# Reordering the start of a fused retention and MLP kernel, and moving its crossbar transposes to another queue

## The chip, the cores and the metric

The kernel runs on one core of one Trainium2 chip. The metric is the device time of one execution in microseconds (us), given as the median of several executions of the same kernel. The profile is one execution, taken by the hardware profiler, and all times of day in it count from the start of its span. One thing is needed all through this study: the time of an execution is some 1.7 us more than its span. So spans are compared with spans here, and times with times.

## The reference

```python
def _attn_ref(q, k, v):                     # q, k, v: 8 batches x 8 heads x 576 x 64
    scores = scale * np.matmul(q, k.transpose(0, 1, 3, 2))
    gamma = 1.0 - 2.0 ** (-5.0 - np.arange(H, dtype=np.float32))
    Dmat = np.where(rel >= 0, gamma[:, None, None] ** rel[None, :, :], 0.0)
    return np.matmul(scores * Dmat[None, :, :, :], v)

def _moe_ref(x, w_in, w_out):               # 4608 x 512, 512 x 2048, 2048 x 512
    h = x @ w_in
    sp = np.where(h > 20.0, h, np.log1p(np.exp(np.minimum(h, 20.0))))
    g = h * np.tanh(sp)
    return (g @ w_out).astype(np.float32)
```

The output of the first function, with heads laid side by side, is the `x` of the second.

## The kernel before

Work comes in **chunks** of 128 tokens; two chunks are a **pair**, four are a **tile** of 512 tokens, and there are 36 chunks. The decay `gamma ** (i - j)` is split into a factor on q and one on v. For a chunk, VectorE scales q (step P), k is cast to bf16 (step C, GpSimd, first tile only), v is scaled (step V, GpSimd in the first tile, VectorE later), q and k are transposed (step T), TensorE makes the scores and VectorE multiplies them by the causal mask (step S), and TensorE multiplies them by v (step O). Then comes the MLP: `g1` multiplies a tile by one of 16 blocks of `w_in` into PSUM, ScalarE applies Mish, and `g2` multiplies by `w_out`.

The start, and the first tile's transposes:

```python
    def load_v(n, queue):
        (b, i0, _), = chunks[n]
        queue.dma_start(out=pairs[n // 2]["v"][:, n % 2], in_=v[b, :, ds(i0, P), :].rearrange("h p d -> p h d"))

    load_v(0, nc.scalar)
    load_v(1, nc.scalar)
    for n in range(NCH):
        load_first(n)              # q and k of chunks 0 to 3, on SyncE's queue
    ...
    keep_warm(13)                  # matmuls on zeros
    ...                            # constants, masks
    load_v(2, nc.gpsimd)
    load_v(3, nc.gpsimd)
    ...
    # step_v: GpSimd for the first tile
        (nc.gpsimd if early else nc.vector).tensor_tensor(r["vs"][:, u], r["v"][:, u], g, op=OP.mult)
    ...
    # step_t
        if n >= NPE:               # pairs 8 to 17: one crossbar transpose each
            nc.scalar.dma_start_transpose(out=r["qk"]..., in_=r["qks"]...)
            return
        if n < NCH:
            tp = ps_h.tile([P, 2, NP, P], BF16, name="hp")
            for i in range(2):     # q, then k
                lines = r["qks"][:, i, u].rearrange("p h d -> p (h d)")
                for t in range(4):
                    nc.tensor.transpose(tp[:, i, t, :], lines[:, ts(t, P)], ident)

                nc.scalar.copy(r["qk"][:, i, u]..., tp[:, i]...)
            return
    ...
    one(0, "PCVT")
    for n in range(NCH):
        last = n == NCH - 1
        keep_warm(4)
        if not last:
            one(n + 1, "P")
        one(n, "S")
        keep_warm(3)
        if not last:
            one(n + 1, "CV")
            if n < 2:
                load_w_in(2 * n, 2)
            one(n + 1, "T")
            one(n, "O")
    load_w_in(4, 4)                # the third piece: blocks 4 to 7 of w_in
    load_w_in(8, 4)
    ...
    for f in range(2):
        g1_some(0, f, NCH - 1)     # "the first projection": blocks 0 to 3, 128x384 matmuls
    one(3, "O")
    for f in range(2, 4):
        g1_some(0, f, NCH - 1)
    g1_chunk(3, 0)
    for i in range(4, nF):         # "block 4" and on: the first 128x512 matmuls
        ...
        g1(0, i)
```

The part near 126 us, in the third tile:

```python
    for i in range(nF):
        visit(6 + i // 8, i % 8)
        if i == 12:
            step_p(8)
            step_v(8)
        elif i == 14:
            cross(8)               # the first crossbar transpose
            load(11)
        g1(2, i)
        ...
```

## Time and profile before

| | before |
|---|---|
| time, median of 3 executions | 320.09 us (320.02 to 320.3) |
| span of the profiled execution | 320.1 us |
| TensorE busy | 306.9 us, 96% |
| first score matmuls | 9.02 us |
| first projection begins | 22.58 us |
| block 4 begins | 26.61 us |
| TensorE's longest wait after that | 2.19 us, at 127.96 |
| from the last matmul to the end | 3.32 us |

TensorE decides. It is nearly always busy once the first projection has begun, so what can be saved is the time before that, and single holes. The "block 4" row is the one to keep: everything before it is start, everything after it is an almost unbroken stream of matmuls, so what block 4 gains is what the start gains. Two more of the kernel before are used later: the stretch from 0 to 6 us (start and end, length, busy time of PE, PEld, DVE, ACT and POOL with counts, granted clock, share of transfer time, GB/s), and the durations in ns (shortest, median, longest) of the crossbar transposes on ScalarE's queue.

```profile
0.00:6.00 6.00, 4.45 (x13) 1.56 (x13) 3.09 (x27) 3.24 (x6) 3.92 (x16) 1.00 0.75 184
```

```profile
L268 ACTq DMA_TRANSPOSE qkT<-qks x10: 1332/1932/6815, 110.7 to 248.7; - x10
```

### The profile page before, as it was taken

The numbers are of one execution on the slowest core, as the hardware profiler recorded it, in microseconds if no ns is written. First come the engines' busy times: TensorE is split into PE (matmuls) and PEld (weight loads), VectorE is DVE, ScalarE is ACT, GpSimd is POOL, SyncE is SP. The second block draws the span as 40 slices with busy tenths as digits, with TensorE's granted clock in tenths as the row PEclk, the third lists the DMA queues.
The fourth block names the chain that finished last, engine by engine and source line by source line (L and its number), as shares of the span: only waits on it lengthen the run. The fifth ranks groups of instructions, "written<-read, shape, count | busy, mean of one in ns | idle before, by whom it ended". The sixth has DMA issues, their size and how long they took to land.

```text
span 320.1 us, 6094 instructions
## 1 busy us (share of the span) xinstructions
PE 306.9 (96%) x2649; PEld 160.1 (50%) x2649; DVE 131.9 (41%) x173; ACT 126.2 (39%) x208; POOL 82.1 (26%) x104
## 2 busy tenths in 40 slices
PE   6689999999999997999999999999999999999995
PEld 2345578745555553444545454445454544444444
DVE  4540555047647672353544444453535332001111
ACT  4347676412555541324434343434242422323200
POOL 6697573533440040404131312240000000000000
PEclk9999999999999999999999999999999999999999
DMA  8889999999997069597995959495040400000022
GB/s 205 213 126 226 200 202 218 203 217 236 223 245 114 16 148 156 124 181 134 211 174 123 168 127 186 112 174 125 33 100 33 100 33 35 33 34 35 33 77 87
DMA packets 73866, 43.38 MB, mean 136 GB/s; under 512 B 57712, under 2 KB 65136, under 8 KB 73840
## 3 DMA queue, kind: packets, MB, share of 16 engines
q0 software_dynamic: 43264, 25.69, 54.4%
q1 hardware_dynamic: 7552, 11.41, 11.5%
q10 hardware_dynamic: 23024, 5.90, 11.3%
q8 instruction: 20, 0.33, 0.4%
q14 instruction: 6, 0.05, 0.0%
HBM read 36.70 MB, written 9.44 MB: 144 GB/s over the span
## 4 chain that ended last, share of the span: by engine, by line
PE 90%; ACT 2%; DMA 2%; ACTq 2%; DVE 1%; SPq 1%; issue 0%; DVEq 0%
PE hp L370 33%; PE ops L408 31%; PE hp L408 6%; PE hp L393 4%; PE sc L306 3%; PE sc L355 3%; DMA qraw<-in_q_dram 2%; PE sc L348 2%; ACTq L268 2%; PE st L327 2%; PE ops L158 2%; PE sc L285 2%; PE hp L420 1%; SPq L138 1%; ACT qkT L286 1%; PE hp L381 1%
## 5 line engine op out<-in xcount | busy, mean ns | idle before, releaser
L370 PE MATMUL hp<-xT,w_in_t 128*128 128x512 bf16 x496 | 126.4, 380 | 2.2 <-ACT gT L372 2.2
L372 ACT ACTIVATE gT<-hp 128x512 bf16<-128x512 f32 x124 | 73.9, 598 | 131.7 <-PE hp L370 119.5
L408 PE MATMUL ops<-w_out_t,gT 128*128 128x512 bf16 x480 | 121.9, 379 | 0.0
L408 PEld LDWEIGHTS <-gT 128*128 128x128 bf16 x560 | 54.3, 98 | 64.6 <-issue 0.8
L428 DVE COPY res<-ops 128x512 f32<-128x512 f32 x30 | 20.8, 692 | 131.3 <-PE ops L408 131.3
L370 PEld LDWEIGHTS <-w_in_t 128*128 128x128 bf16 x496 | 46.0, 98 | 55.4 <-issue 3.0
L309 DVE TENSOR_TENSOR sm<-sc,mask 128x1024 bf16<-128x1024 f32 x36 | 42.7, 1218 | 20.5 <-PE sc L306 20.5
L535 POOL COPY seen<-qkT 1x1 bf16<-1x1 bf16 x10 | 1.8, 176 | 128.4 <-DMA qkT<-qks 128.4
L331 ACT ACTIVATE ssb<-st,diag 128x512 bf16<-128x512 f32 x32 | 20.2, 684 | 12.7 <-PE st L327 12.7
L359 DVE CAST xT<-sc 128x512 bf16<-128x512 f32 x32 | 20.8, 686 | 6.7 <-PE sc L355 5.9
L107 POOL DMA_DIRECT2D qraw<-in_q_dram x16 | 17.2, 1074 | 23.0 <-DVE qks L242 11.9
L259 DVE TENSOR_TENSOR vs<-vraw,gv 128x1024 bf16<-128x1024 f32 (+1 forms) x18 | 19.8, 1101 | 0.0
L242 DVE TENSOR_TENSOR qks<-qraw,gq 128x1024 bf16<-128x1024 f32 (+1 forms) x18 | 19.7, 1097 | 0.0
L408 PE MATMUL hp<-w_out_t,gT 128*128 128x512 bf16 x80 | 18.8, 380 | 0.0
L107 POOL DMA_DIRECT2D qks<-in_k_dram x16 | 17.3, 1083 | 5.2 <-DMA qraw<-in_q_dram 4.9
L107 POOL DMA_DIRECT2D vraw<-in_v_dram x16 | 17.4, 1090 | 3.7 <-DMA w_out_t<-in_moe_w_out_dram 1.6
L393 PE MATMUL hp<-xT,w_in_t 128*128 128x128 bf16 x272 | 16.7, 219 | 0.0
L286 ACT COPY qkT<-sc 128x1024 bf16<-128x1024 bf16 x12 | 12.1, 1014 | 11.7 <-PE sc L285 11.7
L393 PEld LDWEIGHTS <-w_in_t 128*128 128x128 bf16 x272 | 15.4, 98 | 0.7 <-issue 0.2
L355 PE MATMUL sc<-sm,vs 128*64 128x128 bf16 x288 | 13.8, 220 | 0.0
L158 PE MATMUL ops<-idle 128*128 128x512 bf16 x41 | 11.9, 424 | 1.3 <-DVE line L177 1.3
L306 PEld LDWEIGHTS <-qkT 64*128 64x128 bf16 x288 | 8.1, 94 | 9.6 <-issue 5.1
(68 smaller groups left out, 154.9 us busy)
## 6 DMA issues: line engine op xcount, KB each, us to landing
out_dram<-res SPq DMA_DIRECT2D x31, 256.0 KB, 3.3
qraw<-in_q_dram POOLq DMA_DIRECT2D x12, 512.0 KB, 6.6
vraw<-in_v_dram POOLq DMA_DIRECT2D x12, 512.0 KB, 9.7
qks<-in_k_dram POOLq DMA_DIRECT2D x12, 256.0 KB, 7.4
vraw<-in_v_dram POOLq DMA_DIRECT2D x10, 256.0 KB, 8.3
qraw<-in_q_dram POOLq DMA_DIRECT2D x8, 256.0 KB, 9.7
w_out_t<-in_moe_w_out_dram POOLq DMA_DIRECT2D x4, 512.0 KB, 11.9
qraw<-in_q_dram SPq DMA_DIRECT2D x8, 128.0 KB, 4.9
```

Source lines behind the costliest of these rows:

```text
L107: nc.gpsimd.dma_start(out=t[ds(off, ni)].rearrange("p u h d -> p (u h) d"), in_=src[ds(b, 2), :, ds(i0, ni), :].rearrange("b h p d -> p (b ...
L242: nc.vector.tensor_tensor(r["qks"][:, 0, u], r["q"][:, u], g, op=OP.mult)
L259: (nc.gpsimd if early else nc.vector).tensor_tensor(r["vs"][:, u], r["v"][:, u], g, op=OP.mult)
L309: nc.vector.tensor_tensor(sm.rearrange("p e n i -> p (e n) i"), sc.rearrange("p e n i -> p (e n) i"), (mask if len(chunks[n]) == 1 else ma ...
L331: nc.scalar.activation(ssb[:, :, :, e, :], st, AX.Copy, scale=diag[:, e:e + 1])
L355: nc.tensor.matmul(ot[ds(64 * e, 64), p, :], lhsT=vs[:, u, 2 * p + e, :], rhs=sm[:, e, p, :], start=(start and p == 0), stop=True, skip_gr ...
L359: (nc.scalar.copy if t == 0 else nc.vector.tensor_copy)(xts[t][:, :, ts(s, P)], ot)
L370: nc.tensor.matmul(hp, lhsT=w_in_t[:, c, ts(f, P)], rhs=xts[t][:, c, :], start=(c == 0), stop=(c == KC - 1))
L372: nc.scalar.activation(gts[t][:, f, :], hp, AX.Mish)
L393: nc.tensor.matmul(hp[:, j, :], lhsT=w_in_t[:, c, ts(4 * fb + j, P)], rhs=xts[t][:, c, ts(s, P)], start=(c == 0), stop=(c == KC - 1))
L408: nc.tensor.matmul(ops, lhsT=gts[t][:, f, ts(s, P)], rhs=w_out_t[:, f, :], start=(f == 0), stop=(f == nF - 1))
L428: copy(ot, ops)
```

## The change

Its intent is to shorten the start, by bringing q and k sooner and tightening the chain of each of the first chunks, and to free ScalarE's queue of crossbar transposes.

```diff
-    def load_v(n, queue):
+    def load_v(n):
...      # always nc.gpsimd now
-    load_v(0, nc.scalar)
-    load_v(1, nc.scalar)
...
-    keep_warm(13)
+    keep_warm(11)
...      # constants
+    load_v(0)
...      # masks
-    load_v(2, nc.gpsimd)
-    load_v(3, nc.gpsimd)
+    load_v(1)
...      # step_t
-            nc.scalar.dma_start_transpose(
+            nc.sync.dma_start_transpose(
...
                 for t in range(4):
                     nc.tensor.transpose(tp[:, i, t, :], lines[:, ts(t, P)], ident)
+            for i in range(2):
                 nc.scalar.copy(...)
...
-    one(0, "PCVT")
+    one(0, "PC")
+    load_v(2)
+    one(0, "VT")
     for n in range(NCH):
-        keep_warm(4)
+        keep_warm(3)
...
-        keep_warm(3)
+        keep_warm(2)
         if not last:
-            one(n + 1, "CV")
-            if n < 2:
-                load_w_in(2 * n, 2)
-            one(n + 1, "T")
+            one(n + 1, "C")
+            if n == 0:
+                load_v(3)
+            elif n == 1:
+                load_w_in(0, 2)
+            else:
+                load_w_in(2, 2)
+            one(n + 1, "VT")
             one(n, "O")
...      # third tile
-        if i == 12:
+        if i == 6:
             step_p(8)
             step_v(8)
-        elif i == 14:
+        elif i == 8:
             cross(8)
             load(11)
```

More of the change, by code (lines that the diff above doesn't have):

```diff
@@ L139, in load_first @@
                                   in_=heads[b, e, :, ds(i0, P), :].rearrange("p (g t) d -> g p (t d)", t=4))
-    def load_v(n, queue):
+    def load_v(n):
         (b, i0, _), = chunks[n]
-        queue.dma_start(out=pairs[n // 2]["v"][:, n % 2], in_=v[b, :, ds(i0, P), :].rearrange("h p d -> p h d"))
-    load_v(0, nc.scalar)
-    load_v(1, nc.scalar)
+        nc.gpsimd.dma_start(out=pairs[n // 2]["v"][:, n % 2], in_=v[b, :, ds(i0, P), :].rearrange("h p d -> p h d"))
     for n in range(NCH):
@@ L267, in step_t @@
         if n >= NPE:
-            nc.scalar.dma_start_transpose(out=r["qk"].rearrange("p i u n t -> p (i u n) t"),
+            nc.sync.dma_start_transpose(out=r["qk"].rearrange("p i u n t -> p (i u n) t"),
                                           in_=r["qks"].rearrange("p i u h d -> p (i u h d)"))
```

## The prediction

> **What bounds the kernel now.** I first read the page's busy shares and the row of slices: TensorE is busy 306.9 of 320.1 us, nine tenths or more in every 8 us slice but the first three (6, 6, 8 tenths) and the one from 120 us (7), at full granted clock. So only TensorE's idle time, and filler on it, can be gained. The view of waits for TensorE names that idle time:
>
> ```profile
> PE 306.9 (96%) x2649; PEld 160.1 (50%) x2649; DVE 131.9 (41%) x173; ACT 126.2 (39%) x208; POOL 82.1 (26%) x104
> ...
> PE hp L276 <- ACT qkT L278: 2.7, 4, 0.7
> PE hp L276 <- DVE qks L238: 2.4, 2, 1.4
> PE hp L370 <- ACT gT L372: 2.2, 1, 2.2
> PE ops L158 <- DVE line L177: 1.3, 1, 1.3
> ```
>
> The rest of that list is 1.3 us in pieces of at most 0.3. Behind the first two lines stand the first four chunks (up to 22.6 us, where the first projection starts); behind the third stands one event near 126 us. From 24.4 us on TensorE idles only 3.5 us until its last matmul at 316.8 us, 2.2 of them that event; then 3.3 us of final copy and store follow. The start is seen in the chain of waits of the first 24 us and TensorE's timeline there (start, duration, what):
>
> ```profile
> 4.12 6.57 DMA qraw<-in_q_dram
> ...
> 11.54 0.40 PE L276 MATMUL hp<-ident,qks 128*128 128x128 bf16 x4 [1.37 <-DVE qks L238]
> 12.61 0.38 PE L276 MATMUL hp<-ident,qks 128*128 128x128 bf16 x4 [0.67 <-ACT qkT L278]
> 12.92 0.41 PE L355 MATMUL sc<-sm,vs 128*64 128x128 bf16 x8
> 13.27 1.04 PE L158 MATMUL ops<-idle 128*128 128x512 bf16 x4
> 14.24 0.40 PE L306 MATMUL sc<-qkT 64*128 64x128 bf16 x8
> 14.57 0.82 PE L158 MATMUL ops<-idle 128*128 128x512 bf16 x3
> 15.23 0.39 PE L276 MATMUL hp<-ident,qks 128*128 128x128 bf16 x4
> ...
> 18.90 0.39 PE L276 MATMUL hp<-ident,qks 128*128 128x128 bf16 x4
> ...
> 22.58 1.46 PE L381 MATMUL hp<-xT,w_in_t 128*128 128x384 bf16 x8
> ```
>
> Chunk 1's q, issued at 4.12, lands only at 10.70: nothing but bytes ahead of it in the transfers. After that a chunk takes a fixed 3.68 us (15.23 to 18.90): eight transposes in two halves with a 0.67 us wait for the first copy, the output, seven idle matmuls, the scores. The event at 126 us is seen in ScalarE's timeline and TensorE's:
>
> ```profile
> 120.45 6.82 ACTq L268 DMA_TRANSPOSE qkT<-qks  x1
> 127.31 1.08 ACT L372 ACTIVATE gT<-hp 128x512 bf16<-128x512 f32 x2 [6.40 <-issue]
> 127.96 1.02 PE L370 MATMUL hp<-xT,w_in_t 128*128 128x512 bf16 x4 [2.19 <-ACT gT L372]
> ```
>
> ScalarE's queue sat 6.82 us on one crossbar transpose while a pair's loads ran; the activations behind it came late and TensorE ran out of PSUM. The other nine took 1.3 to 4.4 us and left no gap.
>
> **What the Trainium skill says.** *DMA: Bandwidth & Descriptors*, section "Issuing engines are not separate DMA queues": transfers from ScalarE, SyncE and GpSimd run on the same 16 engines and interleave. The trace agrees: v of chunks 0 and 1 (ScalarE's queue, landed 3.98 and 5.83) and v of 2 and 3 (GpSimd's, issued 3.08 and 4.12, landed 8.88 and 10.87) share the time with q and k from SyncE. So another queue makes no bandwidth; only the order counts. The same page, "Silent corruption: two transposing streams in flight at once", forbids mixing queues for transposes; all ten move together, so nothing is mixed (no run shows the corruption). *SBUF — State Buffer*, "Who interferes with whom": a VectorE tensor_tensor with both inputs in SBUF contends with GpSimd's reads. The trace shows q's scaling (128x512) at 0.69 us alone, 1.22 and 1.70 us beside GpSimd's v scaling. *TensorE: Matmul & The Clock Gate*, Part 1: the array starts at half clock until about 3.4 us of activity. The trace: idle matmuls 0.42 us apart from 1.26 to 4.23 us, about 0.22 after.
>
> **Part 1, loads of v.** By 10.7 us some 2 MB have been asked for ahead of or beside q of chunk 1: all four v (1 MB) and q, k of chunk 0 and q of 1 (0.75 MB), plus beginnings of k of 1. In the window 2.8 to 10.7 us that is about 260 GB/s. After: v0 first, v1 only after the masks (about 4 us), v2 and v3 after the casts of chunks 0 and 1. Ahead of q1 then stand q0, k0, v0, itself and a part of v1, about 1.15 MB: 4.4 us from 2.8, so about 7.2 us instead of 10.7. SyncE's issues of 0.65 us per half put q1's end of issue at 4.73, so it can't be much earlier. For chunk 0: q0 lands near 5, scaled at about 5.2 (VectorE's constants end at 5.26) against 6.02; k0 near 5.8 against 6.75. First scores at about 8.35 against 9.02. With the second half of chunk 1's transposes at 9.2 instead of 12.61, chunk 1's scores come at about 11.1 instead of 14.23.
>
> **Part 2, transposes ahead of copies, fewer idle matmuls.** New chunk, counted from its scores: scores 0.33, two idle 0.43, eight transposes 0.5, then output, which waits for the mask product: 0.44 + 1.22 + 0.05 = 1.7 after the scores began; output 0.34; three idle 0.65: 2.7. The other branch: transposes start at 0.76, end with latency at 1.4, both copies 2 x 0.59, release 0.17: 2.75. Both allow about 2.75 against 3.68. GpSimd's branch: cast 0.62, one DMA issue 0.9, v scaling 1.04 (1.49 when it meets VectorE): 2.6 to 3.0 a chunk, now nearly the same size. I take 2.75 to 3.0. Scores of chunk 3: 11.1 + 2 x 2.75..3.0 = 16.6 to 17.1 (21.59 before); first projection 0.87 later: 17.5 to 18.0 against 22.58, so 4.6 to 5.1 us earlier. The idle matmuls removed (10) are inside this sum, not beside it.
>
> **Part 3, can the weights keep up?** GpSimd's casts, scalings and issues end at about 5.8 + 4 x 0.62 + 4 x 1.04..1.25 + 4 x 0.9 = 16.0 to 16.9, where it issues the third w_in piece (18.38 before; it landed 5.4 us later, and was needed at 26.6). New landing 21.4 to 22.3; TensorE now wants it at 26.6 - 4.85 = 21.75. A stall of 0 to 0.5. Later loads come some 2 us earlier and TensorE 4.6 earlier, so each needs 2.6 us of slack: v of chunk 6 landed 40.04 for a scaling at 43.38 (3.3), v of 5 4.0, q of 5 and 6 5.4 and 4.6, the next pairs 9 us and more. So it holds, barely. **Start: 4.6 us gained.**
>
> **Part 4, crossbar transposes on SyncE's queue.** ScalarE is no longer blocked: the 2.19 us gap goes, also for a second reason: the first transpose and its load go from step 14 to step 8, so that load has landed before the second transpose. SyncE then sits on transposes, and stores behind it wait up to 7 us; a store comes every 6.9 us with three result buffers, so it costs nothing. The earlier scaling of pair 8 falls where VectorE idled 1.39 and 0.99 us between masks and copies; the copies come about 1 us later with 4.7 us until someone needs their buffers. **2.2 us gained.**
>
> Sum: 320.1 - 4.6 - 2.2 = **313.3 us**, 2.1% less.
>
> **Rivals.** (a) Transfers take over: w_in lands late. For it: transfers are busy eight or nine tenths from 0 to 96 us, and slack at the third piece is only 2.8 us plus what GpSimd gains. If GpSimd issues no earlier than before, the start gains only about 2.8: 315.1 us. Against it: GpSimd waited 5.0 us for k in the old start, which goes. (b) The pitch of a chunk becomes GpSimd's or VectorE's because the two collide on SBUF: 3.3 us instead of 2.8 costs 1 us: 314.3 us. (c) Transposes on SyncE block behind stores, arrive late, and the scores wait: up to 2 us at each of ten places. Against it: a transpose is issued ahead of its step's store and used some 9 us later, and took 4.3 us to land in most cases; unlikely. (d) The clock falls with fewer idle matmuls. Gaps of 1.37 us left no slow matmuls before (four transposes 0.40 us on both sides of it), and new gaps are shorter. (e) Better: casts begin sooner and the start gains 5.5: 312.4 us.
>
> **Range and chances.** The 2% line is 313.69 us, only 0.4 us above my number. Part 4 is nearly sure. The start carries the spread: plus 0.7, minus 2. I choose 313.3 with 312.2 to 315.2. Faster by over 2%: 0.55, because most of my cases (4.2 us or more at the start) fall on that side; within 2%: 0.44; slower: 0.01.
>
> **What the new profile would show.** q of chunk 1 scaled near 7.5 us, not 10.8; scores of chunks 1 to 3 at about 11.1, 13.9, 16.8; no wait of a transpose for a copy; the first projection near 17.7; GpSimd's third w_in issue near 16.5 and a wait of at most 0.5 us at the first 128x512 matmuls; no gap over 0.4 us after 24 us; ScalarE's 6.40 us hole gone; last matmul near 310. Wrong would be: TensorE waiting for w_in or for activations after it, transposes waiting for GpSimd's casts at every chunk, or gaps at scores of late pairs behind SyncE's queue.

## The result, and the profile after

The changed kernel took a median of **316.75 us** (316.62 to 316.85, 4 executions) against 320.05 (319.77 to 320.3) of the kernel before in the same rounds: ratio 0.9897, interval 0.988 to 0.9914. It is 1.0% faster, which at the 2% line counts as the same. A ratio here is the mean time of one kernel's fast runs over that of the other's of the same rounds, so it is not quite the ratio of the medians. Executions over 1.5% slower than the fastest of the same kernel are left out of the means.

| | before | after | predicted |
|---|---|---|---|
| span of the profiled execution, us | 320.1 | 315.1 | 313.3 |
| q of chunk 1 landed | 10.70 | 7.52 | 7.2 |
| k of chunk 0 landed | 6.75 | 6.81 | 5.8 |
| scores of chunks 0 to 3 | 9.02, 14.24, 17.92, 21.59 | 9.17, 12.30, 15.46, 18.32 | 8.35, 11.1, 13.9, 16.8 |
| first projection | 22.58 | 19.09 | 17.5 to 18.0 |
| third `w_in` piece issued, landed | 18.38, 23.80 | 18.27, 23.89 | 16.5, 21.4 to 22.3 |
| block 4 | 26.61 | 23.94 | 22.0 |

(The predicted 22.0 for block 4 is 26.61 less the 4.6 us.) TensorE's matmuls and their waits from 7 us on, after the change (start, duration, engine, line, what; in brackets the idle time before it and what ended it):

```profile
9.17 0.40 PE L305 MATMUL sc<-qkT 64*128 64x128 bf16 x8 [0.52 <-ACT qkT L277]
...
12.30 0.40 PE L305 MATMUL sc<-qkT 64*128 64x128 bf16 x8
...
13.23 0.87 PE L274 MATMUL hp<-ident,qks 128*128 128x128 bf16 x8
...
15.46 0.40 PE L305 MATMUL sc<-qkT 64*128 64x128 bf16 x8
...
19.09 1.46 PE L380 MATMUL hp<-xT,w_in_t 128*128 128x384 bf16 x8
...
23.94 1.90 PE L369 MATMUL hp<-xT,w_in_t 128*128 128x512 bf16 x8 [0.66 <-ACT gT L394]
```

The chunk's pitch fell to 3.13, 3.16 and 2.86 us, and from chunk 2 on the transposes run as eight in a row: no wait for the first copy is left between them. But the scores come 0.82 us late already at chunk 0, and the pitch is over the predicted 2.75 to 3.0 in two of three chunks. What sets it is seen on VectorE and GpSimd:

```profile
7.62 2.40 DVE L236 TENSOR_TENSOR qks<-qraw,gq 128x512 bf16<-128x512 f32 x1 [1.26 <-DMA qraw<-in_q_dram]
9.94 1.21 DVE L308 TENSOR_TENSOR sm<-sc,mask 128x1024 bf16<-128x1024 f32 x1
11.08 2.09 DVE L236 TENSOR_TENSOR qks<-qraw,gq 128x512 bf16<-128x512 f32 x1
13.09 1.21 DVE L308 TENSOR_TENSOR sm<-sc,mask 128x1024 bf16<-128x1024 f32 x1
14.23 1.80 DVE L236 TENSOR_TENSOR qks<-qraw,gq 128x512 bf16<-128x512 f32 x1
```

```profile
6.95 0.60 POOL L246 CAST qks<-kraw 128x512 bf16<-128x512 f32 x1 [1.48 <-DMA kraw<-in_k_dram]
7.50 0.89 POOL L143 DMA_DIRECT2D vraw<-in_v_dram  x1
8.41 1.05 POOL L257 TENSOR_TENSOR vs<-vraw,gv 128x512 bf16<-128x512 f32 x1
10.04 0.61 POOL L246 CAST qks<-kraw 128x512 bf16<-128x512 f32 x1 [0.58 <-DMA kraw<-in_k_dram]
...
15.40 1.09 POOL L246 CAST qks<-kraw 128x512 bf16<-128x512 f32 x1
...
18.27 1.54 POOL L123 DMA_DIRECT2D w_in_t<-in_moe_w_in_dram  x2
```

q's scaling, 0.69 us when alone, takes 1.80 to 2.40 us beside GpSimd's issue and scaling of v. From 7.62 us on, VectorE goes from scaling to mask to scaling without a pause, and the chain of waits of this execution runs over it from there to 17.2 us. GpSimd starts late: its first cast waits for k of chunk 0 until 6.95, where the prediction counted from 5.8, it waits 0.81 us more for k of chunks 1 and 2, and two casts take 0.80 and 1.09 us instead of 0.61. So the third `w_in` piece is issued no earlier than before, and lands 1.6 us or more after the predicted time. The 0.66 us in front of block 4 is put down to an activation in TensorE's row, but the weight load of the same matmul waited 0.83 us for `w_in`; the piece landed at 23.89, the matmul began at 23.94. Where nothing waits there, block 4 follows the first projection by 4.03 us (22.58 to 26.61 before); here it took 4.85.

The other half of the change did what was expected. ScalarE near the place of the old hole, the transposes on SyncE's queue, and TensorE's waits over the whole span (waiter and releaser: total us, times, longest):

```profile
119.38 0.60 ACT L371 ACTIVATE gT<-hp 128x512 bf16<-128x512 f32 x1 [1.13 <-PE hp L369]
122.29 0.60 ACT L371 ACTIVATE gT<-hp 128x512 bf16<-128x512 f32 x1 [2.31 <-PE hp L369]
```

```profile
L266 SPq DMA_TRANSPOSE qkT<-qks x10: 1317/1911/2003, 100.6 to 242.6; - x10
```

```profile
PE hp L274 <- POOL qks L246: 1.0, 2, 0.8
...
PE hp L369 <- ACT gT L394: 0.7, 1, 0.7
```

In this stretch every activation now waits for TensorE and not the reverse; no transpose holds a queue for more than 2.0 us; and the only 128x512 projection that waits is the one of the start.

From span to span the gain is 5.05 us where 6.8 was predicted. At block 4 it is 2.67 (26.61 to 23.94) instead of 4.6; after block 4 it is 2.53 instead of 2.2 (2.34 at the hole, 0.19 near 143 us); the end after the last matmul grew by 0.14 (3.32 to 3.46). But the medians differ by 3.3 us only. The profiled execution of the kernel before had a time of 321.84 us, 1.8 above that kernel's median, so its span of 320.1 is not the span of an execution of 320.09 us; that the two numbers look alike is chance. Of the eleven executions of that kernel which ran beside the first group of experiments, nine had spans of 317.5 to 318.6. The 5.05 us of the two profiles, less the 1.75 (321.84 less 320.09) by which the first of them was slow, are the 3.3 us of the medians.

### The profile page after: what moved, and what is told of

Same layout as the page of the kernel before. It is cut to its first block, busy times and chain, and to the rows that moved or that the text cites. A ratio compares the mean times of both kernels' runs of the same rounds, so it can differ in the third digit from the quotient of the medians.

```text
span 315.1 us, 6075 instructions
## 1 busy us (share of the span) xinstructions
PE 305.9 (97%) x2639; PEld 159.2 (51%) x2639; DVE 134.2 (43%) x173; ACT 126.3 (40%) x208; POOL 84.2 (27%) x106
## 4 chain that ended last, share of the span: by engine, by line
PE 91%; DVE 4%; ACT 1%; DMA 1%; SPq 1%; issue 1%; DVEq 0%
PE hp L369 34%; PE ops L407 32%; PE hp L407 6%; PE hp L392 4%; PE sc L305 3%; PE sc L354 3%; PE sc L347 2%; PE st L326 2%; DVE qks L236 2%; PE sc L284 2%; PE hp L419 1%; DVE sm L308 1%; DMA qraw<-in_q_dram 1%; SPq L138 1%; ACT qkT L285 1%; PE hp L380 1%
## 5 line engine op out<-in xcount | busy, mean ns | idle before, releaser
L107 POOL DMA_DIRECT2D qraw<-in_q_dram x16 | 17.2, 1076 | 15.2 <-DVE qks L240 7.1
L107 POOL DMA_DIRECT2D qks<-in_k_dram x16 | 17.2, 1079 | 8.3 <-DMA qraw<-in_q_dram 3.8
L354 PE MATMUL sc<-sm,vs 128*64 128x128 bf16 x288 | 13.9, 220 | 0.6 <-DVE sm L308 0.5
L305 PE MATMUL sc<-qkT 64*128 64x128 bf16 x288 | 11.9, 218 | 1.3 <-ACT qkT L285 0.8
```

What stands on the lines that cost most here:

```text
L107: nc.gpsimd.dma_start(out=t[ds(off, ni)].rearrange("p u h d -> p (u h) d"), in_=src[ds(b, 2), :, ds(i0, ni), :].rearrange("b h p d -> p (b ...
L305: nc.tensor.matmul(sc[:, e, p, :], lhsT=qk[r, 1, u, p, :], rhs=qk[r, 0, u, p, :], start=True, stop=True)
L354: nc.tensor.matmul(ot[ds(64 * e, 64), p, :], lhsT=vs[:, u, 2 * p + e, :], rhs=sm[:, e, p, :], start=(start and p == 0), stop=True, skip_gr ...
```

## The experiments

Each kernel was checked against the reference and timed beside the kernel before on the same chip. Where not said otherwise the result was correct. Before any of it ran, what each theory expects was written down. "Block 4" in the tables is when it began in the one profiled execution, and scatters by some tenths; the medians decide.

### Was the kernel before profiled in a usual execution, and what is each half worth?

Four kernels. In the texts, theory A is that the hole near 126 us is there in every execution, theory B that it was an accident of the profiled one. `again` is the kernel before, unchanged. `sp_only` and `early_only` are the kernel before with one half of the transposes' change each; `start_only` is the changed kernel with both halves taken back.

```diff
# sp_only, against before
-            nc.scalar.dma_start_transpose(
+            nc.sync.dma_start_transpose(
# early_only, against before
-        if i == 12:
+        if i == 6:
-        elif i == 14:
+        elif i == 8:
# start_only, against after: both of these undone
```

> The kernel before, unchanged. Its profiled execution took 321.84 us by the clock that times runs, against 320.05 in the median run, so its trace may hold something that most runs lack. Theory A (the 2.2 us hole near 126 us behind a crossbar transpose in ScalarE's queue comes in every run): span about 320.1 and the hole again. Theory B (the hole is an accident of the profiled execution): span 318.0 to 318.6, no gap of TensorE over 0.5 us near 126 us. Time in both 320.0, ratio 1.000.

> The kernel before with one word changed: the ten crossbar transposes from SyncE's queue instead of ScalarE's. Theory A: 2.2 us less, 317.8. Theory B: 0 to 0.7 us less, 319.4 to 320.0.

> The kernel before with pair 8 scaled and transposed at steps 6 and 8 instead of 12 and 14, transposes still from ScalarE. Theory A: the load of pair 11 lands before the second transpose, so the 2.2 us go here too, 317.8 to 318.5. Theory B: within 0.5 us of 320.0. If the early transpose meets the loads that still run near 100 us, a new hole instead: up to 322.

> The changed kernel with its start alone; transposes from ScalarE at the old steps. The traces of before and after put the start's gain at 2.66 us (24 us into the run). Expected by both theories 317.4, with 0.7 us (B) or 2.2 us and more (A) left to the changed kernel's 316.75 -- A can't hold if this gives 317.4 and the changed kernel 316.75.

| kernel | median us (range) | ratio to before, interval | block 4 | second transpose: start, us on the queue | hole behind it |
|---|---|---|---|---|---|
| again | 319.81 (319.48 to 320.05) | 0.9988, 0.9965 to 1.0012 | 25.28 | 119.12, 5.99 | 1.36 |
| sp_only | 318.36 (318.03 to 320.76) | 0.996, 0.9926 to 0.9995 | 25.66 | 118.61, 3.48 | none |
| early_only | 318.14 (318.08 to 318.47) | 0.9939, 0.9916 to 0.9962 | 25.79 | 119.62, 2.21 | none |
| start_only | 318.32 (317.61 to 319.19) | 0.9945, 0.9919 to 0.9971 | 24.47 | 118.30, 6.36 | 1.74 |

An execution of the kernel before can also start differently. In `again`, TensorE's wait at the hole, VectorE's scaling of q in chunk 1, and GpSimd's issue of the third `w_in` piece:

```profile
PE hp L370 <- ACT gT L372: 1.4, 1, 1.4
```

```profile
8.68 0.69 DVE L238 TENSOR_TENSOR qks<-qraw,gq 128x512 bf16<-128x512 f32 x1 [1.95 <-DMA qraw<-in_q_dram]
```

```profile
16.93 1.56 POOL L123 DMA_DIRECT2D w_in_t<-in_moe_w_in_dram  x2
```

q of chunk 1 is scaled at 8.68, not at 10.79 as in the execution that the prediction worked from, and block 4 starts 1.33 us earlier. That time scatters: with the same loads it was 9.38 in `sp_only`, 9.97 in `early_only` and 11.02 in `t_ahead` (below). So the prediction's late q is not a mark of that one execution, but it stands near the late end. The hole is no accident: it recurs in `again`, in `start_only` and in `t_ahead`, but as 1.36, 1.74 and 1.6 us, not 2.19. Either half of the transposes' change alone takes it away, so the two do the same work twice. The last two columns fit with that: at the early position the second transpose holds even ScalarE's queue for only 2.21 us; at the old position it holds SyncE's for 3.48 us, but there no activation stands behind it. By the medians a half is worth 1.5 to 1.8 us (319.9 to 318.36 and 318.14), the start is worth 1.6 (319.9 to 318.32), and the two add up to about the 3.3 us of the whole. Both theories had put `start_only` at 317.4; it missed that by 0.9 us, and three of its six executions have a mean clock of 0.993 to 0.995 (see rival (d) below).

### Theories of the late third piece and of the slow scalings

Four changes to the changed kernel. `w4_first` tests that GpSimd's late issue makes the piece late (theory G): it issues the third piece ahead of the last scaling of v. `v_dve` gives the first tile's v scaling to VectorE, so that only GpSimd's casts of k can still run beside q's scaling. `v_rows` loads v in rows of 1 KB (four times longer; the heads then come in a wrong order, relative error 0.57). Its output is wrong, which doesn't matter for the time. `idle_back` restores the number of idle matmuls.

```diff
# w4_first, against after
             else:
                 load_w_in(2, 2)
+                load_w_in(4, 4)
             one(n + 1, "VT")
...
-    load_w_in(4, 4)
# v_dve, against after
-        (nc.gpsimd if early else nc.vector).tensor_tensor(r["vs"][:, u], ...)
+        nc.vector.tensor_tensor(r["vs"][:, u], ...)
# v_rows, against after: load_v in two loads, as load_first does
+        for e in range(2):
+            nc.gpsimd.dma_start(out=...[:, n % 2, ds(4 * e, 4), :]..., in_=heads[b, e, :, ds(i0, P), :]...)
# idle_back, against after: keep_warm(11), (3), (2) back to 13, 4, 3
```

> The changed kernel with GpSimd issuing the third piece of w_in (the 1 MB one, needed by the fifth block of the first projection) right after the second, ahead of the last chunk's v scaling. Theory G (GpSimd's order sets when that piece lands, and it is what TensorE waits for at 23.9 us): the piece lands about 1 us earlier, TensorE's 0.66 us gap there goes, 316.1 us (ratio 0.9875). Theory P (the pace of the chunks alone sets the start): no change, 316.75 (0.9897), or the last chunk's output comes 0.8 us later and the time is 317.2.

> The changed kernel with the first four v scalings on VectorE instead of GpSimd. If it is the collision of GpSimd's v scaling with VectorE's q scaling on SBUF that stretches the latter from 0.69 to 1.8-2.4 us and so sets the 3.1 us pitch, q scalings fall to 0.7-1.3 us; GpSimd is free 1.05 us a chunk sooner, so the third piece of w_in is issued at 16 to 16.5 instead of 18.3 us. Theory G with collision: 315.0 to 315.5 us (ratio 0.985). Rival (transfers of k and v set the pace, k of chunk 3 lands at 14.7 whatever the engines do): start gains at most 0.7, 316.1.

> The changed kernel with v of the first four chunks loaded in 1 KB rows, as q and k are, instead of 256 B rows. The values then stand in the wrong places: a wrong result on purpose, the same bytes and the same work. In the trace a v of 256 KB holds up the stream 1.9 us against 0.7 for q or k. If rows and not bytes are the cost, k of chunk 0 lands at 5.7 instead of 6.8, k of chunk 3 at 11 to 12 instead of 14.7, GpSimd starts its chain 1.1 us earlier: third w_in piece at 17.1, 315.6 us (0.986). If only bytes count: no change. It issues eight loads from GpSimd instead of four, which costs up to 0.9 us a chunk of its time; that could eat the gain.

> The changed kernel with the idle matmuls of before (13, then 4 and 3 a chunk). If the removal gave time: 0.43 us a chunk on TensorE's own path, up to 1.7 us more, 318.4 (0.995). If TensorE waits for w_in at 23.9 us anyway, or the idle matmuls fill waits for VectorE: under 0.5 us, 316.8 to 317.2. If fewer idle matmuls let the clock fall in some executions (start_only's profile has a granted clock of 0.91 between 6 and 24 us), the spread shrinks and the clock is 1.000 in every run.

| kernel | median us (range) | ratio, interval | scalings of q, chunks 1 to 3 | third piece issued, landed | block 4 |
|---|---|---|---|---|---|
| after, first profile | 316.75 (316.62 to 316.85) | 0.9897, 0.988 to 0.9914 | 2.40, 2.09, 1.80 | 18.27, 23.89 | 23.94 |
| w4_first | 318.76 (317.39 to 320.81) | 0.9959, 0.9919 to 0.9999 | 2.17, 2.30, 2.23 | 17.67, 25.83 | 25.87 |
| v_dve | 316.82 (315.85 to 319.52) | 0.9896, 0.9853 to 0.994 | 0.69, 0.68, 1.10 | 16.02, 24.31 | 24.36 |
| v_rows | 316.9 (316.41 to 317.32) | 0.989, 0.9863 to 0.9918 | 0.69, 0.68, 2.44 | 17.82, 23.23 | 24.06 |
| idle_back | 317.7 (317.53 to 318.38) | 0.9919, 0.9892 to 0.9947 | 2.35, 2.43, 2.77 | 18.03, 23.86 | 24.70 |

`w4_first` missed: the piece was issued 0.6 us earlier and landed 1.9 us later, and TensorE waited 0.42 and then 1.68 us for `w_in`. So the time of issue does not decide by itself when the piece lands.

`v_dve` did what it should to the scalings, and nothing that shows to the time (its interval, 0.9853 to 0.994, would hide some tenths). Its scalings of q, then TensorE's first projection and block 4, and the transfer in the chain of waits over the first 25 us:

```profile
7.30 0.69 DVE L236 TENSOR_TENSOR qks<-qraw,gq 128x512 bf16<-128x512 f32 x1 [0.79 <-DMA qraw<-in_q_dram]
...
11.43 0.68 DVE L236 TENSOR_TENSOR qks<-qraw,gq 128x512 bf16<-128x512 f32 x1
```

```profile
18.99 1.46 PE L380 MATMUL hp<-xT,w_in_t 128*128 128x384 bf16 x8
...
24.36 1.90 PE L369 MATMUL hp<-xT,w_in_t 128*128 128x512 bf16 x8 [1.17 <-DMA w_in_t<-in_moe_w_in_dram]
```

```profile
16.02 8.29 DMA w_in_t<-in_moe_w_in_dram
```

The long scalings are gone, which shows that GpSimd's scaling of v made them long. Its issue of a load does not: in `v_rows` q of chunk 1 was scaled in 0.69 us from 7.59, beside an issue (7.38 to 8.46) and just ahead of the scaling of v (8.46), while in the changed kernel it began at 7.62, the scaling of v at 8.41, and it took 2.40. So about a tenth of a microsecond can decide whether the two meet. The pitch of chunks 2 and 3 became 2.82 us, as predicted. But that of chunk 1 was 3.71: there TensorE waited 1.00 us for the cast of k, which had landed at 10.23. The prediction worked out q of chunk 1, and not k. GpSimd issues the third piece at 16.02, even earlier than predicted, but the transfer then takes 8.29 us instead of the 5.62 of the changed kernel, and 1.17 us of waiting stands in front of block 4. By the trace's transfer records, 14 of the piece's 16 completions were in by 21.8 us and the last two came from 23.2 on; the trace does not name the transfer engines.

`v_rows` gives no sign that v's short rows are the cost: k of chunk 0 landed at 6.70, not at 5.7; its four additional issues could hide a small gain. `idle_back` is 0.8 to 0.9 us slower than `v_dve` and `v_rows` of its rounds (317.7 against 316.82 and 316.9), but only 0.2 to 0.5 slower than later runs of the changed kernel (317.48 and 317.25). So fewer idle matmuls are worth 0 to 0.9 us, and the intervals overlap. As its text expected for that case, no execution of `idle_back` has a mean clock under 0.999.

### Is moving v worth anything?

In the texts, theory M is that moving v carries part of the gain, theory S that it does not. `v_before` is the changed kernel with v's loads and `w_in`'s positions as before. `v0_act` has only the first load of v back on ScalarE's queue. `t_ahead` is the kernel before with the transposes ahead of the copies and nothing else. `after_again` is the changed kernel, unchanged.

```diff
# v0_act, against after
-    def load_v(n):
+    def load_v(n, queue=nc.gpsimd):
+    load_v(0, nc.scalar)           # ahead of the loads of q and k
-    load_v(0)                      # after the constants
# t_ahead, against before
+            for i in range(2):
                 nc.scalar.copy(...)
# v_before, against after: every load_v and load_w_in back in its old place and queue
```

> The changed kernel with the first four v loads where they were: two from ScalarE's queue at the start, two from GpSimd's after the masks, w_in pieces after the v scalings of chunks 1 and 2. The rest of the change stays. Theory S (moving v slows the start of the transfers: in the first 6 us they move 142 GB/s after the change against 184 to 189 before, and it lengthens GpSimd's chain, so the third w_in piece lands at 23.9 instead of 22.5): GpSimd issues that piece by 17.0, it lands at 22.5 to 23, and the time is the changed kernel's or up to 0.8 us less, 316.0 to 316.75 (ratio 0.9873 to 0.9897). Theory M (moving v is what gains, as predicted, since q of chunk 1 lands 1 to 3 us sooner): 318.0 and more (0.994).

> The changed kernel with the very first v load alone put back on ScalarE's queue, where it starts 0.7 us earlier and fills transfers that SyncE's issues leave idle. Theory S: transfers of the first 6 us rise to 165 GB/s or more, v0 lands by 4.5 instead of 6.1, k of chunk 1 by 9.3 instead of 9.9, third w_in piece issued 0.5 us sooner; 316.0 to 316.5. Theory M: no effect or slower, since v0 again stands ahead of q and k of chunk 0: 316.75 to 317.5.

> The kernel before with all eight transposes of a chunk ahead of both copies, and nothing else. Removes four waits of 0.67 us from TensorE's order; the other branch (copies end 1.18 us after the transposes, then the scores) stays, so of 3.68 us a chunk about 0.4 to 0.7 go: 1.3 to 2 us by the first projection, all of it kept because w_in lands early enough (22.5): 318.3 (0.9945). If transfers set the pace, under 0.5 us.

> The changed kernel unchanged, beside the others on the same chip: 316.75 (0.9897), and in its trace a wait of TensorE for w_in at 23 to 25 us of 0.3 to 1.2 us (it was 0.66). If that wait is absent, w_in is not what limits the start.

| kernel | median us (range) | ratio, interval | block 4 | third piece issued, landed |
|---|---|---|---|---|
| v_before | 316.34 (316.13 to 317.73) | 0.9876, 0.9848 to 0.9904 | 24.45 | 17.47, 23.99 |
| v0_act | 316.79 (316.45 to 317.21) | 0.9879, 0.9851 to 0.9907 | 24.47 | 17.62, 24.42 |
| t_ahead | 318.96 (318.82 to 319.71) | 0.9949, 0.9926 to 0.9972 | 25.31 | 18.03, 23.54 |
| after_again | 317.48 (317.01 to 321.52) | 0.9925, 0.988 to 0.9969 | 24.18 | 17.94, 23.52 |

Moving v, the first part of the change, gains nothing: without it the kernel is as fast (316.34 against 317.48, intervals that overlap), and theory M's 318.0 did not come. Theory S was right about the time and wrong about the third piece, which landed at 23.99 and not by 23. What it does to the transfers is seen in the first 6 us of the changed kernel and of `v_before`:

```profile
0.00:6.00 6.00, 4.74 (x11) 1.49 (x11) 3.30 (x28) 3.34 (x6) 4.03 (x16) 1.00 0.52 142
```

```profile
0.00:6.00 6.00, 4.30 (x11) 1.41 (x11) 3.11 (x27) 3.25 (x6) 3.93 (x16) 1.00 0.75 183
```

With v off ScalarE's queue, 142 GB/s flow instead of 183, and the transfers are busy 52% instead of 75% of the time. SyncE's queue hands out 128 KB per 0.65 us in the traces; the estimate from these two numbers is that it alone feeds some 200 GB/s at most. By the trace, GpSimd issued the first v at 1.47 us, and it landed at 6.08 instead of 3.98, in the middle of q and k of chunk 0 instead of ahead of them; k landed right behind it at 6.81. `v0_act` confirms where that time went: with this one load back on ScalarE's queue, k of chunk 0 landed at 5.60 and the first scores came at 7.97, better than the prediction's 5.8 and 8.35. The first 6 us moved only 153 GB/s, though, where theory S had 165 or more. And the start ended no earlier, because TensorE then waited 0.61 and 1.15 us for `w_in`.

`t_ahead` has a pitch of 3.03 us instead of 3.68, and gains 1.6 us in its rounds (320.54 to 318.96). That is as much as the whole start is worth by `start_only` (1.6 us). By these two, what the start gained is the transposes ahead of the copies; whether the idle matmuls add a small part is not shown.

`after_again` did not do what its text expected. TensorE's first projection and block 4:

```profile
20.15 1.46 PE L380 MATMUL hp<-xT,w_in_t 128*128 128x384 bf16 x8
...
24.18 1.89 PE L369 MATMUL hp<-xT,w_in_t 128*128 128x512 bf16 x7
```

Block 4 follows the first projection by 4.03 us, so nothing waited for `w_in`, which had landed at 23.52; by that text, `w_in` is then not what limits the start. The chunks were slower instead: the scaling of q in chunk 3 took 2.71 us (1.80 in the first profile), and the pitch was 3.77 (2.86). A third profile, `after_pair` (below), is like it: 3.02 and 3.96 us, and 4.13 us from the first projection to block 4. So the 0.8 us of waiting for `w_in` belongs to the first of three profiles, and in the other two the pace of the chunks held block 4 as far back.

### Two ceilings

Each repair so far ran into the other limit. So one kernel takes the wait for `w_in` away by other data, and one takes both away: blocks 2 to 7 of the first tile use the columns of the first piece, which is there early. Their outputs are wrong, which doesn't matter for the times. (Relative error 0.168, the work is the same.) Then two correct kernels carry repairs: `v0_split` is `v0_act` with the third piece in two halves, `v0_dve_split` adds `v_dve`.

```diff
# after_reuse, against after; v_dve_reuse has v_dve too
-            nc.tensor.matmul(hp, lhsT=w_in_t[:, c, ts(f, P)], ...)
+            nc.tensor.matmul(hp, lhsT=w_in_t[:, c, ts(f % 2 if t == 0 and f < 8 else f, P)], ...)
# v0_split, against v0_act
-    load_w_in(4, 4)
+    load_w_in(4, 2)
+    load_w_in(6, 2)
```

> The changed kernel, in which the first eight blocks of the first projection take the columns of the first w_in piece, so that TensorE waits for no later piece before block 8 (a wrong result on purpose; all loads stay). If the landing of w_in sets the start: 0.7 us less than the changed kernel, ratio 0.9875 or below. If the pace of the chunks sets it (q scalings of 1.8 to 2.7 us beside GpSimd's v scalings): no change, 0.989 to 0.991, first 128x512 block at 23.3 to 24.2 us.

> The same with the v scalings on VectorE, so that neither the collision nor w_in holds TensorE up. If there are two ceilings of nearly the same height (v_dve alone showed a wait for w_in of 1.17 us in place of the collision), both gone give 1.2 us and more: 315.3 to 315.7, ratio 0.985, first 128x512 block at 22.5 to 23.3 us. If neither matters (the pace is set by k's landing): 0.989.

> v0_act with the third w_in piece (1 MB) loaded as two of 0.5 MB, a right result. Blocks 4 and 5 then need only the first half, which should land 1.2 us earlier; v0_act's trace had waits for w_in of 0.61 and 1.15 us. If w_in is v0_act's ceiling: 1 us less than v0_act, 315.6 (0.985). If another issue on GpSimd's queue delays what follows, or the chunks' pace takes over: 316.5 and more.

> All three repairs in one right kernel: first v load on ScalarE's queue, v scalings of the first four chunks on VectorE, third w_in piece in halves. If transfers at the start, the collision and the landing of w_in are the three things that kept the start from the predicted 4.6 us: 314.8 to 315.5 (ratio 0.983). If transfers alone bound it: as v0_split.

| kernel | median us (range) | ratio, interval | block 4 |
|---|---|---|---|
| after_reuse | 317.13 (316.88 to 317.18) | 0.9915, 0.9903 to 0.9928 | 24.35 |
| v_dve_reuse | 315.88 (315.72 to 316.12) | 0.9878, 0.9866 to 0.9891 | 23.03 |
| v0_split | 316.25 (315.56 to 317.01) | 0.9893, 0.9876 to 0.9911 | 22.39 |
| v0_dve_split | 316.46 (315.39 to 317.11) | 0.9895, 0.9879 to 0.9912 | 22.43 |

Taking the wait for `w_in` away alone shows no gain (317.13; the unchanged partner did not run in these rounds, but the ratio of 0.9915 lies among its 0.9897, 0.9901 and 0.9925): scalings of 2.38 and 2.70 us then set block 4 at 24.35. Taking the long scalings away alone showed none either (`v_dve`, 316.82, in other rounds): `w_in` then set it at 24.36. Taking both away gains 1.25 us over the first (317.13 to 315.88, intervals apart). Over `v_dve` the gain rests on the traces, for there the intervals overlap (0.9878 and 0.9896). In the trace of `v_dve_reuse` block 4 follows the first projection at once:

```profile
19.00 1.46 PE L380 MATMUL hp<-xT,w_in_t 128*128 128x384 bf16 x8
...
23.03 1.89 PE L369 MATMUL hp<-xT,w_in_t 128*128 128x512 bf16 x8
```

Its first projection begins at the same moment as that of `v_dve` (19.00 and 18.99); block 4 is 1.33 us apart, which is the wait for `w_in`. So the start has two ceilings at nearly one height, 24.35 and 24.36, and the next lies 1.3 us lower: a repair of one alone shows no gain.

`v0_split`, a correct kernel, brings k and `w_in` sooner and leaves the scalings of v on GpSimd; those of q took 0.69, 1.06 and 1.80 us. Block 4 came at 22.39, the earliest of all, 1.55 us before that of the changed kernel, yet its last matmul was only 0.80 us earlier (310.82 against 311.62). Part of it is given back at a later wait. TensorE's row and VectorE's:

```profile
37.74 0.40 PE L305 MATMUL sc<-qkT 64*128 64x128 bf16 x8 [0.79 <-DVE xT L358]
```

```profile
36.39 0.69 DVE L257 TENSOR_TENSOR vs<-vraw,gv 128x512 bf16<-128x512 f32 x1 [0.98 <-DMA vraw<-in_v_dram]
37.00 0.68 DVE L358 CAST xT<-sc 128x512 bf16<-128x512 f32 x1
```

VectorE's queue stood on v of a later chunk, and the copy that TensorE needed stood behind it. This is the third limit in a row, and again transfers. `v0_dve_split`, with all three repairs, missed its 314.8 to 315.5: its median is 316.46, no better than `v0_split`. Its profiled execution, 315.39 with block 4 at 22.43, is the fastest of six, so it does not stand for the others.

### Is the better version real?

The last two runs are the changed kernel and `v0_split`, unchanged, on the same chip.

> The changed kernel once more, as the partner on one chip of split_pair: 316.8 to 317.3, ratio 0.990 to 0.9915.

> v0_split once more beside the changed kernel on the same chip. If w_in's landing and the early transfers together were a ceiling of the changed kernel: 0.6 to 1.0 us less than its partner, 316.0 to 316.5, ratio 0.988 to 0.9895. If the start's gain is given back later (its trace had a wait of 0.79 us for a VectorE copy near 37 us): within 0.3 us of its partner.

`after_pair` took 317.25 us (316.9 to 317.34; 0.9901, 0.9884 to 0.9917) and `split_pair` 316.66 (315.85 to 317.14; 0.9884, 0.9866 to 0.9901). That is 0.2% better with ranges that overlap: a hint, not a settled gain. In `split_pair` the wait for the copy to xT was 0.56 us, at 38.3.

## Why the prediction was right or wrong

The prediction said 313.3 us, in 312.2 to 315.2; the result is 316.75. It put 0.44 on "within 2%", which is what came.

- **What bounds the kernel: the views were read rightly, but one slow execution was taken for the usual one.** The first term of the sum, "320.1 - 4.6 - 2.2", is both a span and nearly the median time, and the prediction took them for the same. The span belonged to an execution of 321.84 us. So about 1.75 us of what its profile offered (block 4 at 26.61 instead of 25.3 to 25.8, a hole of 2.19 instead of 1.36 to 1.74) was not there to be gained in a usual execution. That is half of the miss of 3.45 us. The other half is in the spans themselves, 5.05 us gained instead of 6.8, and the start is to blame for it (2.67 instead of 4.6; after block 4 0.3 more was gained than predicted, the end took 0.1). The 1.93 us that the start fell short are, term by term: first scores 0.82 us late; three pitches of 9.15 us together where the prediction's longer case has 8.75, 0.40; 0.82 for the wait for `w_in`; less 0.10, since the first projection came 0.77 us after the last scores and not 0.87. (The row of slices was read with one slip: its last slice is a 5 as well, which the 3.3 us of the end explain.)
- **Part 1 (q of chunk 1 at 7.2, k of chunk 0 at 5.8, first scores at 8.35): right for q, wrong for k, and worth nothing.** q came at 7.52. k came at 6.81, because the first v, which the prediction kept "first", left its place ahead of k when it changed queues; with it back, k came at 5.60. The step that failed is "another queue makes no bandwidth; only the order counts": the first 6 us moved 142 GB/s with v off ScalarE's queue and 183 with it there (`v_before`). k of chunk 1 was left out of the sum; it landed at 9.92, and the second half of chunk 1's transposes came at 10.71 instead of 9.2. And `v_before`, without this part, is as fast.
- **Part 2 (2.75 to 3.0 us a chunk): the mechanism was right, a term was mis-sized.** The transposes' wait is gone. The prediction allowed 1.49 us for v's scaling "when it meets VectorE", on GpSimd, and left VectorE's own cost of the meeting out of the sum; it had put 1.22 and 1.70 us beside q's scaling itself. It measured 1.80 to 2.40, and up to 3.02 in other executions. The pitch became 3.13, 3.16 and 2.86, in others up to 3.96 (`after_pair`, chunk 3). This is rival (b), whose 3.3 us a chunk was about right. `v_dve` and `v_dve_reuse` show the cause for chunks 2 and 3, whose pitch fell to 2.82; chunk 1 stays at 3.71 and 3.49 there, behind k.
- **Part 3 (third piece issued near 16.5, landing 21.4 to 22.3): this step failed.** It was issued at 18.27 and landed at 23.89, and TensorE waited 0.8 us instead of "0 to 0.5". The sum counted GpSimd's chain from k of chunk 0 at 5.8 and without a wait; it began at 6.95 and waited 0.81 us for k on the way. Rival (a) had the size: "If GpSimd issues no earlier than before, the start gains only about 2.8"; the start gained 2.67 from span to span. (That its 315.1 us is also the span after is in part luck: the pace of the chunks and the wait for `w_in` both enter.) Its reading was incomplete, though: when GpSimd did issue at 16.02 (`v_dve`), the piece landed at 24.31 all the same. And in the three other profiles with the start of the kernel before it was issued at 16.93 to 17.31, against 17.94 to 18.27 in the three of the changed kernel, so the change made it later, by 0.6 us or more.
- **Part 4 (2.2 us for the hole): right in kind**, 2.34 us in the profiles; in usual executions 1.5 to 1.8. The second reason given, that the load moves earlier, is enough by itself. Rival (c), that SyncE's queue would block behind stores, did not come: no transpose took over 2.0 us in the changed kernel.
- **Rival (d), the clock.** The prediction called it unlikely, and fewer idle matmuls did no harm in the medians (0 to 0.9 us gained). But the clock did dip in three profiled starts, `start_only`, `v_rows` and `v_before`, all with fewer idle matmuls, so it is not ruled out as part of the scatter. By the recorded mean clocks such executions are also more frequent: of those in the fast state, 13 of 72 with fewer idle matmuls have 0.995 or less, and 4 of 82 with the old number. They are not always slow, but the three slowest of the kernel before beside the experiments (321.93 to 322.81 us, 0.994) are all among them (the profiled one of 321.84 us is not: 1.000). That is a hint and no proof. In `start_only`, with the changed start, the granted clock from 6 to 24 us was 0.91 (third number from the end):

```profile
6.00:24.00 18.00, 14.90 (x141) 7.90 (x141) 11.85 (x7) 8.03 (x16) 15.90 (x20) 0.91 0.93 193
```

Left open: why the third piece lands at 23.2 to 24.4 us, or later, for issues from 16.0 to 18.3 in the changed kernel and its variants; why one or two of a piece's 16 completions come 1 to 2.2 us after the others in some runs; and why single executions of several kernels are 2 to 4 us slower (319.52 of `v_dve` and 321.52 of `after_again`, both at a mean clock of 0.995), when an execution of the changed kernel at 0.994 took 316.62 and one of `after_again` at 0.994 took 317.28. None of the runs settles these.

## What to carry to other kernels

Compare the time of the profiled execution with the median before any gap in it is counted as gain: a wait that two executions of the same kernel do not share can't be counted on. When work is moved to bring an engine's chain forward, add the slowdown of both partners where two engines meet, not of one. And where a repair shows nothing, take away the next limit too before calling it useless: here two repairs that each showed no gain gave 1.25 us together.

## What the Trainium skill lacked or had wrong

- *SBUF — State Buffer*, "Who interferes with whom", says that a VectorE instruction with two SBUF inputs contends with a GpSimd instruction that reads SBUF. The runs agree: up to 3.02 us for a q scaling beside GpSimd's v scaling, 0.68 to 1.13 us once that was moved. What it lacks is the size for this pair: the loss can be more than the whole 1.05 us of the instruction met (2.40 instead of 0.69 us), and a cast on GpSimd also took 1.09 instead of 0.61 us.
- *DMA: Bandwidth & Descriptors*, "Issuing engines are not separate DMA queues", calls the issue time that a second issuing engine saves usually small. At this start it was not: with v off ScalarE's queue the first 6 us moved 142 GB/s instead of 183 to 189, and k landed no earlier.
- *DMA: Bandwidth & Descriptors*, "Latency and other measured facts", has engines 7 and 15 usually slower, as a best guess from the descriptor rings of GpSimd's queue. It would fit the last two of 16 completions of the third piece, 1.4 us or more behind the other 14, but the trace does not name the engines, so no run here shows it.
- *TensorE: Matmul & The Clock Gate*, Part 1, has the clock fall after an idle window of about 3.4 us. With fewer idle matmuls the granted clock was 0.91 between 6 and 24 us in three profiled starts, of which one stretch of 2 us (10 to 12 us in `start_only` and `v_rows`, 12 to 14 in `v_before`) was at 0.50; TensorE's longest wait ahead of it was 1.3 us.
- No page says how long a crossbar transpose holds the queue that issues it on this chip while other transfers run (*DMA: Bandwidth & Descriptors* has cycles of the sequencer for one, in a section on trn3 alone). Here it was 1.3 to 6.8 us on ScalarE's, with the activations behind it held up, and 1.3 to 2.0 us on SyncE's after the change (up to 3.48 us in `sp_only`).
